# Values of batch 0 summed by matmul, and the adding transfers of batches 1 and later moved: pooled attention and two MLPs on one core

## The chip, the cores and the metric

The kernel runs on one core of one Trainium2 chip. The metric is device time in microseconds of one execution, the median over runs. In all that follows PE is the tensor engine (PEld its weight loads), DVE the vector engine, ACT the scalar engine, POOL the general engine, which also issues the transfers that add, and SP the engine that issues the other transfers. Every engine works through its own list of instructions strictly in order.

## The reference

```python
# q, k, v: [8, 8, 576, 64]; pool = 8, Sp = 72
k_p = k.reshape(B, H, Sp, pool, D).mean(axis=3)
v_p = v.reshape(B, H, Sp, pool, D).mean(axis=3)
scores = scale * np.matmul(q, k_p.transpose(0, 1, 3, 2))
attn = softmax(scores)
x = np.matmul(attn, v_p)            # tokens 4608 x 512
h = x @ moe_w_in                    # 512 x 2048
x = where(h >= 1, h, where(h <= -1, 0, (h + 1)**2 / 4)) @ moe_w_out
h = x @ moe2_w_in
out = (h / (1 + exp(-h))) @ moe2_w_out
```

All products are made of float16 pairs (a high and a low part, three matmuls each), and the weights come in as 64-bit words.

## The kernel before

The 4608 tokens are worked in nine chunks of 512. A chunk's attention makes x, then 16 slices of h (`emit_h`, twelve matmuls each), then y. Before the first slice of h can be made, `moe_w_in` has to be converted: nine pieces (`cuts1`) are loaded by SP, ACT looks at each (L237), DVE takes its maximum (L238), a matmul with the identity and a DVE reduction (L245, L248) give one scale for the whole of a group of pieces, and DVE (L92, L257, L260), ACT (L263, L265) and POOL (L266) turn a piece into its two halves `wa0` to `wa8`. A piece passes through a scratch tile `xf`, of which there are three, so the fourth conversion on DVE has to wait until POOL is done with the first.

Keys and values are pooled 8 to 1 over the rows of a batch. For batch 0's keys eight transfers bring everything, and DVE sums it (L421). All other sums of a batch (`kv_pool`) begin with a transfer of SP that brings four of the eight rows (`kv_load`, L408) into a tile `raw`, of which there are two; then a transfer issued by POOL brings the other four and adds them in place (`kv_more`, L412); then DVE adds in two steps (L427, L430) and frees `raw`. The text calls batch b's keys and values kb and vb, so v0 is batch 0's values, k1 batch 1's keys. The sums of v0 are needed early: their largest mean (L433, L106, L107) sets the scales `skv` and `tsv`, and with `tsv` ACT and DVE split x (L357, L358) for the first slice of h.

`pool_to`, `more_to` and `load_to` count through the list (k0, v0, k1, v1, ...), four pooling steps each, and are called from the main loop. The order in which an engine gets its instructions is then set by a scheduler, which moves ready work ahead by its own estimate of times; the engines keep to that order whatever the chip's times are. The row numbers of the changed file are 7 to 18 higher in the lines named here (L421 is L428, L427 and L430 are L445 and L448, L412 is L419, L571 is L589).

Of the kernel before, what the change touches and what calls it, by code (L numbers as in the profile page):

```python
# [9 lines left out]
F32 = mybir.dt.float32  # L10
# [22 lines left out]
def tile_pooled_attention_two_mlps(  # L33
# [18 lines left out]
    nc = tc.nc  # L52
    B, H, S, D = q.shape
    NT, DM = out.shape
    DFF = moe_w_in.shape[1]
    POOL = 8
    SP = S // POOL
# [42 lines left out]
    ident = const.tile([128, 128], F32, name="ident")  # L100
# [262 lines left out]
    kvp = att_ctx.enter_context(tc.tile_pool(name="kvp", bufs=4))  # L363
# [23 lines left out]
    def att_ps(shape):  # L387

        n = early["n"] % 6
        early["n"] += 1  # L390
        if early["on"] and n > 1:
            return ps_y.tile(shape, F32, tag=f"y{n - 2}", name="early")
        return ps_a.tile(shape, F32, tag="a", name="att")

    sums, kv_raw, vscale = {}, {}, {}

    def kv_rows(b, which):
        return (k if which == "k" else v)[b].rearrange("h (p r) d -> p h r d", r=POOL)

    def kv_load(b, which):  # L400
        if (b, which) == (0, "k"):
            for h in range(H):
                r = gp.tile([128, 2, N], F16, tag="g", name="k0").rearrange("p a n -> p (a n)").bitcast(F32)
                r = kv_raw[b, which, h] = r[0:SP].rearrange("p (r d) -> p r d", r=POOL)
                nc.sync.dma_start(out=r, in_=k[0, h].rearrange("(p r) d -> p r d", r=POOL))
            return
        r = kv_raw[b, which] = kvp.tile([SP, H, HALF, D], F32, tag="raw", name="raw", bufs=2)
        nc.sync.dma_start(out=r, in_=kv_rows(b, which)[:, :, 0:HALF])  # L408

    def kv_more(b, which):  # L410

        nc.gpsimd.dma_start(out=kv_raw[b, which], in_=kv_rows(b, which)[:, :, HALF:POOL], accum_op=ALU.add)  # L412

    def kv_pool(b, which, j):
        if j == 0:
            sums[b, which] = kvp.tile([SPT, H, D], F32, tag="sum", name="sum", bufs=3)
            if which == "k":
                nc.gpsimd.memset(sums[b, which][SP // 32 * 32:SPT], 0.0)
        if (b, which) == (0, "k"):  # L419
            for h in (2 * j, 2 * j + 1):  # L420
                nc.vector.tensor_reduce(  # L421
                    out=sums[b, which][0:SP, h], in_=kv_raw.pop((b, which, h)).rearrange("p r d -> p d r"),
                    axis=AX.X, op=ALU.add,
                )
        elif j == 2:
            r = kv_raw[b, which]
            nc.vector.tensor_tensor(out=r[:, :, 0:2], in0=r[:, :, 0:2], in1=r[:, :, 2:4], op=ALU.add)  # L427
        elif j == 3:  # L428
            r = kv_raw.pop((b, which))
            nc.vector.tensor_tensor(out=sums[b, which][0:SP], in0=r[:, :, 0], in1=r[:, :, 1], op=ALU.add)  # L430
# [41 lines left out]
    def values_scale(b):  # L472
        pool_to(8 * b + 8)
        if b not in vscale:
            vscale[b] = sums_scale(sums[b, "v"][0:SP], vm, ev[:, b:b + 1], rows(SP))
# [79 lines left out]
    def paced(f, engine="dve"):  # L555

        if engine in late:
            with tc.issue_after(late[engine].ins):
                f()
        else:  # L560
            f()
# [104 lines left out]
    def piece_of(cuts, m):  # L666
        return next(p for p, c in enumerate(cuts) if c[1] >= (m + 1) * 128)
# [105 lines left out]
    def emit_h(s, w, x):  # L773
        if s < KF and (s + 4) % 6 > 1:
            ps = ps_y.tile([128, N], F32, tag=f"y{(s + 4) % 6 - 2}", name="hps")
        else:
            ps = ps_h.tile([128, N], F32, tag="h", name="hps")
        wh, wl = w(s % KF)
        for c in range(KD):
            three(ps, wh[:, c], wl[:, c], x[0][:, c], x[1][:, c], c == 0, c == KD - 1)  # L780
        h_t[s] = ps
# [6 lines left out]
    def pre_A(s, r):  # L788

        w = g32_t[s] = up.tile([128, N], F32, tag="g", name="g32")  # L790
        nc.scalar.activation(out=w, in_=h_t.pop(s), func=AF.Relu, scale=c_A(r, "c1", s), bias=r["br"])  # L791

    def min_A(s, r):
        u_t[s] = up.tile([128, N], F32, tag="u", name="u")
        ts(u_t[s], g32_t[s], r["lim"], op0=ALU.min)

    def mid_A(s, r):
        nc.scalar.activation(out=u_t[s], in_=u_t[s], func=AF.Square, scale=r["rsg"])  # L798

    def post_A(s, r):  # L800

        return nc.vector.scalar_tensor_tensor(  # L802
            out=g32_t[s], in0=g32_t[s], scalar=r["br"], in1=u_t.pop(s), op0=ALU.subtract, op1=ALU.max
        )
# [21 lines left out]
    def split_g(s, r):  # L826
        g = g32_t.pop(s)
        to = slots.pop(0)() if s < KF else gp.tile([128, 2, N], F16, tag="g", name="g16")
        gh, gl = g_t[s] = to[:, 0], to[:, 1]
        nc.scalar.copy(out=gh, in_=g)  # L830
        return nc.vector.tensor_tensor(out=gl, in0=g, in1=gh, op=ALU.subtract)  # L831
# [190 lines left out]
    def batches(i):  # L1022

        b = segs(i)[-1][2]
        if i == NI:
            batch_keys(0)
            batch_values(0)
        if segs(i - 1)[-1][2] != b:
            pool_to(8 * b + 4)
            batch_keys(b)  # L1030
            pool_to(8 * b + 8)
            batch_values(b)
# [13 lines left out]


    kv = [(b, w) for b in range(B) for w in ("k", "v")]
    done = {"load": 0, "more": 1, "pool": 0, "q": 0}

    def load_to(n):
        while done["load"] < min(n, len(kv)):
            kv_load(*kv[done["load"]])
            done["load"] += 1

    def more_to(n):
        load_to(n)
        while done["more"] < min(n, len(kv)):
            kv_more(*kv[done["more"]])
            done["more"] += 1  # L1060

    def pool_to(n):
        while done["pool"] < min(n, 4 * len(kv)):
            u, j = divmod(done["pool"], 4)
            if j == 0:
                more_to(u + 1)
                load_to(u + 2)
            if done["pool"] >= 16:
                paced(lambda: kv_pool(*kv[u], j))
            else:  # L1070
                kv_pool(*kv[u], j)
            if j == 2:
                more_to(u + 2)
            done["pool"] += 1

    def q_to(n):
        while done["q"] < min(n, NTOK):
            load_q(done["q"])
            done["q"] += 1
# [4 lines left out]
    def run(*fs):  # L1084
        for f in fs:
            f()
# [1 line left out]
    load_to(1)  # L1088
    q_to(3)
    load_to(2)  # L1090
    more_to(2)
    q_to(4)
    for p in range(len(cuts1)):
        load1(p)
    load_to(3)
    pool_to(4)
    keys32(0)
    stages = [att_qT, att_scores, att_norm, att_T, att_pv]
    for n in range(NI + len(stages) - 1):
        if n == 2:  # L1100
            pool_to(8)
        for j, f in enumerate(stages):
            if 0 <= n - j < NI:
                f(n - j)
    early["on"] = False
    r = XT[0]
    for a, b in ((0, 3), (3, 7), (7, 9)):
        for p in range(a, b):
# [15 lines left out]
    def slots_to(n):  # L1124
        while left and len(first) - len(left) < n:
            with tc.high_priority(offset=1000):
                left.pop(0)()
                q_to(NI + (len(first) - len(left)) // 4 + 3)
                pool_to(16 + max(0, len(first) - len(left) - 12) * 4 // 6)

    n1 = 1
    for s in range(KF + 2):
        if s < KF:
            while n1 < min(len(cuts1), piece_of(cuts1, s) + 2):
                paced(lambda: convert1(n1), "x")
                n1 += 1
            emit_h(s, chunk1, r["x"])
        z = s - 1
        if 0 <= z < KF:
            pre_A(z, r)  # L1140
            min_A(z, r)
        if 1 <= z:
            split_g(z - 1, r)
        if 0 <= z < KF:
            mid_A(z, r)
            post_A(z, r)
        if s < 8:
            pool_to(9 + s)
        if s == 1:
            q_to(5)  # L1150
            run(*loads2)
        if s >= 9:
            slots_to((s - 8) * 6 // 8)
        if s == 12:
            run(*more2)
            run(*work2[0])
# [127 lines left out]
```

## Time and profile before

| | |
|---|---|
| median of 3 runs | 1670.01 us (1666.96 to 1671.76) |
| profiled execution | 1664.62 us, span 1662.8 us |
| busy share | PE 92%, DVE 73%, ACT 54%, POOL 34% |
| transfers | 166.35 MB, mean 100 GB/s |

The span is what the trace covers. A busy share is a mean over stages of very different kind, so what a change in one stage is worth is read from that stage alone.

### The profile page before, as it was taken

How to read it: one execution, taken by the hardware profiler on the slowest of the kernel's cores; microseconds unless marked ns; L12 is line 12 of the kernel's file. 1: busy time of each engine (PE TensorE's matmuls, PEld its weight loads, DVE VectorE, ACT ScalarE, POOL GpSimd, SP SyncE). 2: the span in 40 equal slices, each digit the busy share in tenths (PEclk: the TensorE clock that was granted, in tenths of full speed). 3: DMA queues.
4: the chain of work that ended last, by engine and by line, in shares of the span. 5: the costliest groups of instructions: out<-in, count | busy, mean ns of one | idle time of the engine just before them, and what ended most of it. 6: DMA issues, size and time to landing. Idle time of an engine off the chain costs nothing.

```text
span 1662.8 us, 34247 instructions
## 1 busy us (share of the span) xinstructions
PE 1531.8 (92%) x14214; PEld 1051.0 (63%) x14214; DVE 1215.3 (73%) x2165; ACT 892.6 (54%) x1417; POOL 570.6 (34%) x494
## 2 busy tenths in 40 slices
PE   4474779989899999999999999999999999999998
PEld 3321334444444444444444469999999999999998
DVE  6499848777667767786776757777777777777765
ACT  3277436465565656675556555445544454445543
POOL 2242321213232433341255514334334343344322
PEclk7587889989999999999999999999999999999999
DMA  9734466964737539354756241100000001000000
GB/s 286 148 104 118 95 141 165 179 147 99 129 114 122 137 79 196 80 136 110 214 212 246 100 177 40 37 27 27 27 34 33 27 27 39 27 27 27 27 15 26
DMA packets 228304, 166.35 MB, mean 100 GB/s; under 512 B 156532, under 2 KB 196340, under 8 KB 228148
## 3 DMA queue, kind: packets, MB, share of 16 engines
q1 hardware_dynamic: 216388, 155.29, 33.8%
q0 software_dynamic: 11760, 8.87, 4.2%
q8 instruction: 111, 1.82, 0.5%
q14 instruction: 45, 0.37, 0.1%
HBM read 102.76 MB, written 33.55 MB: 82 GB/s over the span
## 4 chain that ended last, share of the span: by engine, by line
PE 67%; DVE 14%; DMA 7%; ACT 6%; issue 3%; SPq 2%; POOL 1%; DVEq 0%; ACTq 0%; POOLq 0%
PE hb L119 7%; PE hb L120 7%; PE hb L121 7%; PE y L994 7%; PE y L992 7%; PE y L993 7%; PE y L119 4%; PE y L121 4%; PE y L120 4%; PE hps L119 4%; PE hps L121 4%; PE hps L120 4%; DMA kT<-rows 2%; DVE g L831 1%; DVE u L92 1%
## 5 line engine op out<-in xcount | busy, mean ns | idle before, releaser
L119 PE MATMUL hb<-xh,wc 128*128 128x128 f16 x2016 | 347.7, 219 | 0.0
L121 PE MATMUL hb<-xh,wc 128*128 128x128 f16 x2016 | 347.7, 219 | 0.0
L120 PE MATMUL hb<-xl,wc 128*128 128x128 f16 x2016 | 347.6, 219 | 0.0
L358 DVE SCALAR_TENSOR_TENSOR g<-c,tsg,g 128x512 f16<-128x512 f32 x252 | 228.7, 910 | 80.8 <-ACT g L357 80.8
L992 PE MATMUL y<-wd,g 128*128 128x256 f16 x1008 | 274.8, 273 | 0.0
L994 PE MATMUL y<-wd,g 128*128 128x256 f16 x1008 | 274.8, 273 | 0.0
L993 PE MATMUL y<-wd,g 128*128 128x256 f16 x1008 | 274.8, 273 | 0.0
L119 PE MATMUL hps<-xh,wa 128*128 128x512 f16 x576 | 224.3, 390 | 18.0 <-ACT g L791 10.8
L932 ACT ACTIVATE c<-c,tc 128x512 f32<-128x512 f32 x144 | 103.2, 717 | 228.1 <-DVE c L929 228.1
L119 PE MATMUL y<-g,wb 128*128 128x512 f16 x544 | 209.7, 388 | 16.6 <-ACT wb L210 16.1
L120 PE MATMUL hps<-xl,wa 128*128 128x512 f16 x576 | 224.1, 389 | 0.0
L357 ACT ACTIVATE g<-c,tsg 128x512 f16<-128x512 f32 x252 | 177.6, 718 | 85.7 <-POOL c L695 48.2
L121 PE MATMUL hps<-xh,wa 128*128 128x512 f16 x576 | 221.8, 386 | 1.6 <-POOL wa L266 1.5
L121 PE MATMUL y<-g,wb 128*128 128x512 f16 x544 | 210.5, 387 | 5.5 <-POOL wb L211 5.5
L120 PE MATMUL y<-g,wb 128*128 128x512 f16 x544 | 210.4, 387 | 0.5 <-DVE g L831 0.5
L929 DVE TENSOR_TENSOR c<-c,hb 128x512 f32<-128x512 f32 x252 | 168.8, 682 | 57.5 <-PE hb L121 55.3
L120 PEld LDWEIGHTS <-wc 128*128 128x128 f16 x2016 | 197.1, 98 | 2.4
L119 PEld LDWEIGHTS <-wc 128*128 128x128 f16 x2016 | 197.1, 98 | 2.3
L121 PEld LDWEIGHTS <-wc 128*128 128x128 f16 x2016 | 197.1, 98 | 0.0
L692 POOL TENSOR_TENSOR c<-c 128x512 f32<-128x512 f32 x108 | 164.0, 1532 | 2.8
L802 DVE SCALAR_TENSOR_TENSOR g<-g,tbr,u 128x512 f32<-128x512 f32 x144 | 121.0, 841 | 55.9 <-ACT u L798 55.1
L571 POOL TENSOR_TENSOR e<-e,den 128x576 f32<-128x576 f32 x36 | 52.2, 1450 | 317.0 <-DVE den L570 240.1
(180 smaller groups left out, 2701.1 us busy)
## 6 DMA issues: line engine op xcount, KB each, us to landing
raw<-in_moe_w_out_dram SPq DMA_DIRECT2D x21, 1024.0 KB
raw<-in_moe_w_in_dram SPq DMA_DIRECT2D x18, 1024.0 KB
y<-y SPq DMA_DIRECT2D x36, 256.0 KB
yin<-y SPq DMA_DIRECT2D x18, 512.0 KB
out_dram<-ob SPq DMA_DIRECT2D x36, 256.0 KB
d<-hl SPq DMA_DIRECT2D x32, 256.0 KB
qt<-in_q_dram SPq DMA_DIRECT2D x31, 256.0 KB
wc<-d SPq DMA_DIRECT2D x8, 896.0 KB
```

What stands on the lines that cost most here:

```text
L119: nc.tensor.matmul(out=acc, lhsT=wh, rhs=xh, start=start, stop=False)
L120: nc.tensor.matmul(out=acc, lhsT=wh, rhs=xl, start=False, stop=False)
L121: nc.tensor.matmul(out=acc, lhsT=wl, rhs=xh, start=False, stop=stop)
L357: a = nc.scalar.activation(out=hi, in_=x, func=AF.Copy, scale=s)
L358: return a, nc.vector.scalar_tensor_tensor(out=lo, in0=x, scalar=s, in1=hi, op0=ALU.mult, op1=ALU.subtract)
L692: nc.gpsimd.tensor_tensor(out=out, in0=a, in1=b, op=ALU.subtract)
L802: return nc.vector.scalar_tensor_tensor(out=g32_t[s], in0=g32_t[s], scalar=r["br"], in1=u_t.pop(s), op0=ALU.subtract, op1=ALU.max)
L929: nc.vector.tensor_tensor(out=out, in0=x, in1=y, op=ALU.add)
L932: nc.scalar.activation(out=x, in_=x, func=AF.Silu, scale=r["c1"])
L992: nc.tensor.matmul(out=acc, lhsT=xh, rhs=wh, start=start, stop=False)
L993: nc.tensor.matmul(out=acc, lhsT=xh, rhs=wl, start=False, stop=False)
L994: nc.tensor.matmul(out=acc, lhsT=xl, rhs=wh, start=False, stop=stop)
```

## The change

v0 is now loaded whole by SP, in four transfers into two tiles of the `raw` tag, and 32 matmuls with the identity add up the eight rows in PSUM; ACT copies the result. k1 and v1 are no longer loaded and added during the first chunk's attention: their loads are issued after it (`load_to(4)`), their adding transfers in the loop over the slices of h (`more_to(4)` at s = 1), and their pooling starts at s = 2 in place of 0. For all later batches the adding transfer is asked for one pooling step later.

```diff
         if b == 0:
+            src = v[0].rearrange("h (p r) d -> p h r d", r=POOL)
+            for j in range(2):
+                r = kv_raw[b, which, j] = kvp.tile([SP, 4, POOL, D], F32, tag="raw", name="v0", bufs=2)
+                for i in range(2):
+                    nc.sync.dma_start(out=r[:, 2 * i:2 * i + 2], in_=src[:, 4 * j + 2 * i:4 * j + 2 * i + 2])
+            return
         r = kv_raw[b, which] = kvp.tile([SP, H, HALF, D], F32, tag="raw", name="raw", bufs=2)
...
+        elif b == 0:
+            if j == 0:
+                kv_raw["ps"] = att_ps([SP, H, D])
+            ps, r = kv_raw["ps"], kv_raw[b, which, j // 2][:, j % 2 * 2:j % 2 * 2 + 2]
+            for n in range(POOL):
+                nc.tensor.matmul(
+                    out=ps[:, 2 * j:2 * j + 2], lhsT=ident[0:SP, 0:SP], rhs=r[:, :, n], start=n == 0,
+                    stop=n == POOL - 1,
+                )
+            if j == 3:
+                nc.scalar.copy(out=sums[b, which][0:SP], in_=kv_raw.pop("ps"))
...
-    done = {"load": 0, "more": 1, "pool": 0, "q": 0}
+    done = {"load": 0, "more": 2, "pool": 0, "q": 0}
...
-                load_to(u + 2)
+                load_to(u + 2 if u > 1 else 2)
...
-            if j == 2:
+            if j == 3 and u > 1:
                 more_to(u + 2)
...
     load_to(2)
-    more_to(2)
     q_to(4)
     for p in range(len(cuts1)):
         load1(p)
-    load_to(3)
     pool_to(4)
...
     early["on"] = False
+    load_to(4)
...
     for s in range(KF + 2):
+        if s == 1:
+            more_to(4)
...
-        if s < 8:
-            pool_to(9 + s)
+        if 2 <= s < 10:
+            pool_to(7 + s)
```

Three places show what this does to the order on the engines. The first is DVE at the end of the first chunk's attention, before the change: `raw_189` is k1, `raw_511` is v1, `tsv_337` the scale for x, `xl` the low half of x; what an instruction waits for stands in brackets, DMASW being the adding transfers of POOL.

```order
L107 TENSOR_REDUCE cols_95<-all_350 128x1 [waits PE_49]
L92 TENSOR_SCALAR cols_95<-cols_95 128x1 [waits DVE_49]
L94 TENSOR_SCALAR skv_348<-cols_95 128x1 [waits DVE_49]
L94 TENSOR_SCALAR te_335<-cols_95 128x1
L427 TENSOR_TENSOR raw_189<-raw_189 72x8x128 [waits DMASW1_49]
L94 TENSOR_SCALAR ts_336<-te_335 128x1 [waits DVE_49]
L94 TENSOR_SCALAR tsv_337<-te_335 128x1
L358 SCALAR_TENSOR_TENSOR v160_114<-sum_235,skv_348,v160_114 72x512 [waits Activation_49]
L430 TENSOR_TENSOR sum_513<-raw_189 72x512 [waits DVE_49,Pool_49]
L358 SCALAR_TENSOR_TENSOR xl_346<-early_358,tsv_337,xh_345 128x4x128 [waits Activation_49]
L358 SCALAR_TENSOR_TENSOR xl_346<-early_388,tsv_337,xh_345 128x4x128 [waits Activation_49]
L427 TENSOR_TENSOR raw_511<-raw_511 72x8x128 [waits DMASW2_49]
```

With the change the same scales stand in the middle of the attention, without k1 or v1 between them (DVE, a place some ten instructions earlier).

```order
L94 TENSOR_SCALAR skv_380<-cols_95 128x1 [waits DVE_49]
L94 TENSOR_SCALAR te_367<-cols_95 128x1
L585 TENSOR_SCALAR den_348<-den_348 128x8 [waits DVE_49]
L584 TENSOR_REDUCE den_401<-e_341 128x8 [waits Activation_49]
L94 TENSOR_SCALAR ts_368<-te_367 128x1 [waits DVE_49]
L94 TENSOR_SCALAR tsv_369<-te_367 128x1
```

The first steps of k1 (`raw_467`) and v1 (`raw_469`) now stand together on DVE, behind the conversion of pieces 1 and 2 of `moe_w_in` (the last L260 of which is just ahead of these rows) and ahead of the constants of the first chunk and of piece 3 (DVE again, second place, with the change).

```order
L94 TENSOR_SCALAR cols_95<-cols_95 128x2 [waits DVE_49]
L92 TENSOR_SCALAR cols_95<-cols_95 128x1 [waits DVE_49]
L445 TENSOR_TENSOR raw_467<-raw_467 72x8x128 [waits DMAHW4_49,DMAHW3_49,DMASW0_49]
L445 TENSOR_TENSOR raw_469<-raw_469 72x8x128 [waits DMAHW6_49,DMAHW5_49,DMASW1_49]
L94 TENSOR_SCALAR cols_95<-cols_95 128x2 [waits DVE_49]
L94 TENSOR_SCALAR skv_827<-cols_95 128x1 [waits DVE_49]
L681 TENSOR_REDUCE cols_95<-cols_95 128x1
L94 TENSOR_SCALAR tch_370<-cols_95,te_367 128x9
L448 TENSOR_TENSOR sum_604<-raw_467 72x512 [waits DVE_49,Pool_49]
L448 TENSOR_TENSOR sum_712<-raw_469 72x512 [waits DVE_49]
```

So the waits for k1 and v1 have moved from ahead of `tsv` to behind the first three pieces' conversion. On POOL, the third place, these are the rows between the attention and piece 3 before the change (`raw_624` is k2, `raw_1473` is v2).

```order
L412 DMA raw_189<-in_k_dram 72x8x256 [waits DMAHW6_49]
L418 MEMSET sum_513 16x512 [waits Pool_49]
L412 DMA raw_511<-in_v_dram 72x8x256 [waits DMAHW4_49,DMASW0_49,DVE_49]
L412 DMA raw_624<-in_k_dram 72x8x256 [waits DMAHW5_49,DMASW1_49,DVE_49]
L266 TENSOR_TENSOR wa0_128<-xf_448,wa0_128 128x1024 [waits Activation_49,Pool_49]
L412 DMA raw_1473<-in_v_dram 72x8x256 [waits DMAHW6_49,DMASW2_49,DVE_49]
L266 TENSOR_TENSOR wa1_129<-xf_491,wa1_129 128x1024 [waits DVE_49,Activation_49]
L266 TENSOR_TENSOR wa2_130<-xf_541,wa2_130 128x1024 [waits DVE_49,Activation_49]
```

And these with the change, where `raw_467`, `raw_469`, `raw_710` and `raw_1508` are k1, v1, k2 and v2.

```order
L419 DMA raw_467<-in_k_dram 72x8x256 [waits DMAHW5_49,DMAHW4_49,DMAHW3_49]
L419 DMA raw_469<-in_v_dram 72x8x256 [waits DMAHW6_49]
L266 TENSOR_TENSOR wa0_128<-xf_484,wa0_128 128x1024 [waits Activation_49]
L266 TENSOR_TENSOR wa1_129<-xf_527,wa1_129 128x1024 [waits DVE_49,Activation_49]
L419 DMA raw_710<-in_k_dram 72x8x256 [waits DMAHW1_49,DMASW0_49,DVE_49]
L425 MEMSET sum_1510 16x512 [waits DVE_49,Pool_49]
L266 TENSOR_TENSOR wa2_130<-xf_575,wa2_130 128x1024 [waits Activation_49,Pool_49]
L419 DMA raw_1508<-in_v_dram 72x8x256 [waits DMAHW2_49,DMASW1_49]
```

The adding transfers of k1 and v1 now follow each other at once, and the low halves of pieces 2 and 3 stand behind those of k2 and v2. On SP the loads of k1 and v1 now come behind all of `moe_w_in` and the next four loads of q, and ahead of the first two pieces of `moe_w_out`. Behind this stage POOL's list is the same but for one swap, and PE's list is the same row for row over its last nine tenths.

## Rows read from the trace of the kernel before

**Rows 1.** Busy time by stage: start:end, length, engines busy (instructions), granted clock, DMA share, GB/s.

```profile
0.00:45.00 45.00, 17.77 (x96) 14.45 (x96) 28.14 (x48) 17.39 (x24) 10.32 (x16) 0.76 0.95 278
45.00:60.00 15.00, 4.56 (x22) 3.13 (x22) 1.05 (x5) 2.76 (x7) 2.74 (x3) 0.50 0.91 193
60.00:78.20 18.20, 10.44 (x54) 7.60 (x55) 13.25 (x27) 6.36 (x9) 4.07 (x3) 0.50 0.58 113
78.20:118.60 40.40, 32.35 (x144) 14.35 (x143) 39.24 (x63) 25.20 (x35) 18.50 (x8) 0.92 0.41 109
118.60:160.00 41.40, 17.57 (x88) 7.26 (x86) 40.65 (x94) 32.29 (x54) 6.17 (x3) 0.75 0.43 119
160.00:215.00 55.00, 42.35 (x261) 18.98 (x262) 42.70 (x70) 26.86 (x38) 22.00 (x15) 0.81 0.49 109
215.00:420.00 205.00, 184.76 (x1187) 88.67 (x1186) 142.54 (x296) 111.55 (x193) 54.57 (x49) 0.94 0.70 143
420.00:1662.80 1242.80, 1221.97 (x12370) 896.56 (x12368) 907.66 (x1569) 670.15 (x1062) 452.25 (x399) 1.00 0.30 84
```

**Rows 2.** Waits of DVE from 40 to 165 us: total, times, longest.

```profile
DVE raw L427 <- DMA raw<-in_k_dram: 12.5, 1, 12.5
DVE cols L107 <- PE all L106: 9.4, 1, 9.4
DVE raw L427 <- DMA raw<-in_v_dram: 4.9, 1, 4.9
```

**Rows 3.** Timeline of DVE: start, duration, instruction, idle before it.

```profile
59.67 1.22 DVE L427 TENSOR_TENSOR raw<-raw 72x1024 f32<-72x1024 f32 x1 [12.51 <-DMA raw<-in_k_dram]
...
68.47 1.22 DVE L427 TENSOR_TENSOR raw<-raw 72x1024 f32<-72x1024 f32 x1 [4.88 <-DMA raw<-in_v_dram]
...
71.14 0.68 DVE L430 TENSOR_TENSOR sum<-raw 72x512 f32<-72x512 f32 x1
...
71.74 0.74 DVE L358 SCALAR_TENSOR_TENSOR xl<-att,tsv,xh 128x512 f16<-128x512 f32 x1
...
72.40 0.67 DVE L238 TENSOR_SCALAR_CACHE_REDUCE wa<-wa 128x512 f32<-128x512 f32 x1
...
78.16 2.16 DVE L92 TENSOR_SCALAR xf<-wa 128x1024 int32<-128x1024 int32 x3
...
80.85 1.21 DVE L257 SCALAR_TENSOR_TENSOR xf<-raw,xf 128x1024 int32<-128x1024 int32 x1
...
83.79 1.21 DVE L260 SCALAR_TENSOR_TENSOR xf<-raw,xf 128x1024 int32<-128x1024 int32 x1
...
86.06 0.41 DVE L248 TENSOR_REDUCE cols<-all 128x2 f32<-128x256 f32 x1
...
118.57 1.21 DVE L180 TENSOR_SCALAR_CACHE_REDUCE xf<-xf 128x1024 f32<-128x1024 f32 x1
```

**Rows 4.** Timeline of ACT: its looks at pieces 5 and 8 of `moe_w_in`.

```profile
34.54 1.14 ACT L237 ACTIVATE wa<-wb 128x1024 f32<-128x1024 f32 x1 [1.47 <-DMA wb<-in_moe_w_in_dram]
...
43.76 1.12 ACT L237 ACTIVATE wa<-wb 128x1024 f32<-128x1024 f32 x1 [2.33 <-DMA wb<-in_moe_w_in_dram]
```

**Rows 5.** Timeline of POOL: it issues the adding transfers of k1 and v1.

```profile
47.62 1.40 POOL L412 DMA_DIRECT2D raw<-in_k_dram  x1 [11.22 <-DMA raw<-in_k_dram]
...
59.18 1.38 POOL L412 DMA_DIRECT2D raw<-in_v_dram  x1 [9.59 <-DMA raw<-in_v_dram]
```

**Rows 6.** Transfers, 46 to 75 us: adding queue's packets, MB, share of 16 engines.

```profile
q0 software_dynamic: 1568, 1.18, 28.7%
```

**Rows 7.** Transfers, 0 to 40 us: issues, count, KB each, us to landing (v0).

```profile
raw<-in_v_dram POOLq DMA_DIRECT2D x1, 576.0 KB, 13.4
```

**Rows 8.** Transfers, 70 to 100 us: the same for k2 and v2.

```profile
raw<-in_k_dram POOLq DMA_DIRECT2D x1, 576.0 KB, 9.9
...
raw<-in_v_dram POOLq DMA_DIRECT2D x1, 576.0 KB, 7.8
```

**Rows 9.** Groups of PE up to 60 us: busy us, mean ns; idle before.

```profile
L453 PE MATMUL att<-ident,sum 72*128 72x72 f32 x4 | 1.4, 360 | 7.6 <-DVE sum L421 7.6
```

More of the change, by code (lines that the diff above doesn't have):

```diff
@@ L406, in kv_load @@
             return
+        if b == 0:
+            src = v[0].rearrange("h (p r) d -> p h r d", r=POOL)
[4 more added lines that the diff above has]
+            return
         r = kv_raw[b, which] = kvp.tile([SP, H, HALF, D], F32, tag="raw", name="raw", bufs=2)
```

## The prediction

> **What bounds the kernel now.** I read the table of stages first [rows 1]. From 420 us on PE is busy 1222 of 1243 us at the full clock; nothing in the change touches that stretch, so it can only start sooner or later. The part ahead of it is where time can be won. Up to 45 us the transfers set the pace (share 0.95): nine pieces of moe_w_in come in, one MB each 3.07 us (pieces 5 to 8, 34.54 to 43.76 [rows 4]). From 45 to 60 us nothing works: DVE is busy 1.05 of 15 us, PE 4.56, ACT 2.76. From 78.2 to 160 us DVE is busy 79.9 of 81.8 us, while PE is busy 49.9: DVE converts the weights, and PE waits for them. So the first 160 us are a chain of loads, then waits, then DVE, and what DVE loses there the whole kernel loses.
>
> Next I read what DVE waited for [rows 2]: 12.5 us for the adding transfer of k1 and 4.9 us for that of v1. Nobody needs k1 or v1 yet; but the wait for k1 stands ahead of tsv in DVE's list, so x, the scales and the conversion of pieces 1 to 8 stand behind it. The third wait, 9.4 us, ends with v0's maximum, shortly after the last piece. The timeline [rows 3] shows the consequence: six maxima (L238) start only at 72.40, although the last piece was read by ACT from 43.76 [rows 4], and the conversion of piece 1 starts at 78.16.
>
> **What the change removes.** By the order, tsv and the four splits of x no longer wait for k1 or v1. With v0 whole at PE in the first 20 us, the attention of chunk 0 goes on as before up to about 40 us, and DVE takes the maxima as the pieces come. From about 40 us it has to do, in this order: four splits of 0.74, six maxima (72.40 to 78.16, 5.8), then what stood from 78.16 to 86.06 and a little behind it, less the half-width piece 3, which now comes later. From the rows: L92 and L248, 78.16 to 80.85 less 0.4 for piece 3, 2.3; two L257 of 1.21, 2.4; two L260, 83.79 to 86.06, 2.3; small ones some 1.5, an estimate [rows 3]. That is 3.0 + 5.8 + 8.5 = 17.3, so DVE stands at about 57.4 us before the first step of k1.
>
> **The wait that it adds.** There DVE waits again: L445 of k1 and of v1 need both adding transfers. When do they land? Half of v0 (0.59 MB) moves from an adding transfer to a plain one. Two adding transfers took 28.7% of sixteen engines over 29 us [rows 6], so 4.2 us each; plain, the same bytes take 1.8 us at 3.07 us per MB [rows 4]. So moe_w_in is in about 2 us sooner, at 41.7. Behind it come four loads of q (0.79 MB) and the halves of k1 and v1 (1.18 MB), 6.0 us at that pace, 47.7; I take 49.5, since SP issues them late. (Before, k1's half was in at 47.62 and v1's by 59.18 [rows 5].) POOL issues in 1.4 us. Alone or in traffic one such transfer took 12.05 us (k1: 47.62 to 59.67), 9.3 (v1: 59.18 to 68.47 [rows 3, 5]), 13.4 (v0 [rows 7]), 9.9 and 7.8 (k2, v2 [rows 8]). Here two run together with one to two MB of moe_w_out: 2 x 4.2 + 3.1 to 6.1 = 11.5 to 14.5 us if all sixteen engines are kept busy. The later one lands at 49.5 + 1.4 + 13 = 64 us. Lower bound: 49.5 + 1.4 + 7.8 = 58.7, beyond which DVE's own 57.4 counts. Upper bound: one behind the other at the largest durations, 50.9 + 12.05 + 13.4 = 76.4. I take 64, as the engines' share in such stretches was 0.91 [rows 1] and so the work, not the latency, decides.
>
> Behind that wait on DVE stand the constants of the chunk (without which ACT can't empty PSUM), batch 0's keys, and pieces 3 to 8; PE meanwhile has the converted pieces 0 and 1 and the high half of piece 2, so it can fill PSUM, but that buys nothing, since DVE is the bound.
>
> The Trainium skill, DMA: Bandwidth & Descriptors, section on the anatomy of one DMA on the SWDGE path, gives 2.0 us plus bytes over 436 GB/s for a transfer issued by GpSimd: 3.4 us for 0.59 MB. The trace disagrees (7.8 to 13.4 us for five adding ones). By that page of the Trainium skill the later one would be in at about 54, ahead of DVE, and the wait would be gone; the sum would give 1647 in place of 1653.
>
> **From the wait on.** A place that both kernels pass in the same state is the first L180, the first maximum of moe_w_out: 118.57 us before [rows 3]. From 78.16 to it passed 40.4 us. With the change the part behind the wait lacks the 7.0 us named above (2.3 + 2.4 + 2.3), and has in addition the first step of v1 and both second steps, 1.22 + 2 x 0.68 = 2.6 [rows 3]; the first step of k1 fits into the wait. That is 36.0. POOL adds something: the low half of piece 2 stands behind k2's adding transfer, whose load can only start when raw is free, some 2.4 us after the landing, and DVE's next use of that xf tile waits for it. The load (1.8 us at the pace of rows 4, and a start), POOL's issue of 1.4 and its own work end about 11 us after the landing, when DVE has come there at about 9. I take 2 us, between 0 (a wait of the size of the idle that the 40.4 us held anyway, 40.40 less 39.24 [rows 1]) and 6 (load and issue in full). So L180 starts at 64 + 38.0 = 102.0 in place of 118.6: **16.6 us sooner**.
>
> **What costs nothing.** 32 matmuls for v0: the nearest row is 360 ns for 72 partitions [rows 9], 11.5 us at most if none overlapped; PE is busy 17.8 of the first 45 us, and all wait for pieces until 43.76. Without that cover up to 11.5 us less whatever lies under v0's own load would show; I take 0. ACT's copy of the sum, under the 1.12 us of rows 4, lies there too. The two DVE steps of v0 (1.9 us) go, from a stretch in which DVE is idle 16.9 of 45 us [rows 1]: 0. The later batches' transfers asked for a step later: POOL's list behind the first stage is the same, so 0; the bounds are a microsecond or two either way.
>
> **What becomes of it.** From 118.6 to 160 us DVE stays full, so all of the gain is handed on. From 160 to 420 us PE is busy 227 of 260 us [rows 1], with waits that come from the conversion and transfers of the same chunks; they move with the rest. Sum: 1664.6 - 16.6 = 1648.0 for the profiled execution. That one lies 5.4 us under the median of the runs shown and 2.3 under the fastest, so I carry the difference over to the median: 1670.0 - 16.6 = **1653 us**.
>
> **Rivals.** All times are medians. (a) *No wait left*: the adding transfers are in by 57.4, or DVE comes there later than I think. Then L180 starts at 57.4 + 38 = 95.4, 23 us sooner: 1647. For it: sixteen engines may be freer than before, and 58.7 is my lower bound; against: not one of the five landed in under 7.8 us. The Trainium skill, on the page cited above, would have it so. (b) *Half is lost later*: in the conversion of moe_w_out (160 to 215 us) DVE is only busy 42.7 of 55 us, so ACT, POOL and loads share the bound, and a shorter start may leave them behind: 8 us left, 1662. Against: the loads of moe_w_out wait for tiles that DVE frees, and so come sooner as well. (c) *No change*: the later adding transfer lands at 76.4, the upper bound; then L180 starts at 114.4, 4 us sooner, 1666, or the later stages eat it all, 1670. For it: 13.4 us in the heaviest traffic [rows 7]. (d) *Slower*: the two adding transfers and the plain loads share the engines so badly that the landing is later than 118.6 - 38.0 = 80.6 us, 31 us after the loads; each us beyond costs one, and from 85.6 the loss is over 0.3%, say 1676. For it: everything of DVE, and by xf and POOL's list everything of POOL, hangs on this one landing; against: it is six us more than the worst sum of rows.
>
> **How the numbers follow.** My case (landing between 60 and 69, 1649 to 1658) has 0.50, (a) 0.18, (b) 0.13, (c) 0.12, (d) 0.07. 0.3%, 5 us, is about what a measurement of this kernel can tell from no change (its three runs span 4.8). The forecast, (a) and (b) are beyond it: faster 0.81, same 0.12, slower 0.07. The range from 1643 (a with some luck behind it) to 1665 (between b and c) leaves out (d), most of (c) and little else.
>
> **What would show it.** Right: no DVE wait for k1 or v1 ahead of the splits of x; the last piece's maximum soon after 44 to 46 us; one wait of DVE for the adding transfer of v1, 4 to 8 us, ending near 64; POOL's low half of piece 2 some 11 us behind it; the first L180 near 102; the stretch behind it as long as before. Wrong: a landing beyond 70, a DVE that arrives much before or after 57, a wait of DVE on POOL over 6 us, or a first L180 that is early and a last PE instruction that is not.

## The result, and the profile after

The changed kernel takes 1652.12 us (median of 4 runs, 1646.63 to 1653.79); the kernel before took 1668.49 beside it (4 runs, 1666.14 to 1671.76). The ratio is 0.9895, with a 95% interval of 0.9864 to 0.9926: 16.4 us faster. The profiled execution took 1653.58 us, its span is 1651.8, so only 11.0 us below that of before; the table at the end of the experiments comes back to the rest.

The changed kernel's table of stages, columns as in [rows 1]:

```profile
0.00:45.00 45.00, 29.41 (x220) 25.32 (x220) 29.53 (x58) 24.68 (x38) 8.55 (x16) 0.89 0.93 281
45.00:60.00 15.00, 3.56 (x14) 2.54 (x14) 13.39 (x29) 1.93 (x2) 2.91 (x2) 0.62 0.98 209
60.00:78.20 18.20, 8.58 (x31) 3.39 (x31) 9.66 (x23) 7.36 (x12) 7.65 (x5) 0.78 0.77 159
78.20:118.60 40.40, 33.75 (x135) 14.57 (x136) 35.24 (x60) 31.11 (x47) 18.04 (x8) 0.86 0.56 140
118.60:160.00 41.40, 18.50 (x105) 8.02 (x104) 37.08 (x78) 29.73 (x47) 8.78 (x5) 0.71 0.36 89
160.00:215.00 55.00, 45.35 (x335) 21.65 (x332) 42.15 (x70) 24.34 (x33) 24.43 (x16) 0.91 0.38 103
```

Against [rows 1] the second line tells most: from 45 to 60 us DVE is busy 13.39 us in place of 1.05. The third gives some of it back, 9.66 in place of 13.25, and in the fourth and fifth DVE is no longer full (72.3 of 81.8 us, 79.9 before). The waits of DVE from 0 to 165 us, columns as in [rows 2]:

```profile
DVE u L92 <- ACT g L809: 7.3, 2, 5.6
DVE raw L445 <- DMA raw<-in_v_dram: 4.5, 1, 4.5
DVE wa L238 <- ACT wa L237: 4.5, 1, 4.5
DVE xl L358 <- ACT xh L357: 4.2, 1, 4.2
DVE xf L180 <- ACT xf L175: 3.2, 1, 3.2
...
DVE raw L445 <- DMA raw<-in_k_dram: 1.6, 1, 1.6
```

The three waits of [rows 2], 26.8 us, have gone from their places; 6.1 us for k1 and v1 stand at the new place, and waits for ACT have come in. DVE's timeline shows where, columns as in [rows 3]:

```profile
35.42 0.14 DVE L94 TENSOR_SCALAR tsv<-te 128x1 int32<-128x1 int32 x1
...
44.63 0.68 DVE L238 TENSOR_SCALAR_CACHE_REDUCE wa<-wa 128x512 f32<-128x512 f32 x1
...
58.08 0.15 DVE L92 TENSOR_SCALAR cols<-cols 128x1 int32<-128x1 int32 x1
59.84 1.22 DVE L445 TENSOR_TENSOR raw<-raw 72x1024 f32<-72x1024 f32 x1 [1.61 <-DMA raw<-in_k_dram]
65.60 2.00 DVE L445 TENSOR_TENSOR raw<-raw 72x1024 f32<-72x1024 f32 x1 [4.54 <-DMA raw<-in_v_dram]
...
80.09 2.61 DVE L92 TENSOR_SCALAR u<-g,tlim 128x512 f32<-128x512 f32 x1 [5.64 <-ACT g L809]
...
107.00 1.22 DVE L180 TENSOR_SCALAR_CACHE_REDUCE xf<-xf 128x1024 f32<-128x1024 f32 x1 [3.19 <-ACT xf L175]
```

tsv is there at 35.42 (60.88 before), the maxima start at 44.63 (72.40 in [rows 3]), DVE is through with the first pieces at 58.2, v1 lands at 65.60, and the first L180 comes at 107.00, 11.6 us sooner than before. What held DVE at 80 us shows in the timeline of ACT:

```profile
77.53 0.63 ACT L451 ACTIVATE rows<-sum 80x512 f32<-80x512 f32 x1 [4.07 <-DMA kT<-rows]
...
79.29 0.76 ACT L809 ACTIVATE g<-hps,tbr,tc 128x512 f32<-128x512 f32 x1
```

ACT takes k1's mean (L451) and writes the output that nobody needs into a `rows` tile, which the transposes of the keys (kT) still read; g, for which DVE waits, stands behind it.

A later common place is the first DVE step on the first chunk's y, which waits for the chunk's last matmul. It comes at 228.92 us before and at 213.04 after:

```profile
228.92 1.41 DVE L92 TENSOR_SCALAR y<-y,cy 128x512 f32<-128x512 f32 x2 [2.40 <-PE y L121]
```

```profile
213.04 1.41 DVE L92 TENSOR_SCALAR y<-y,cy 128x512 f32<-128x512 f32 x2 [2.40 <-PE y L121]
```

There the gain is 15.9 us. The table at the end of the experiments uses this place.

### The profile page after: what moved, and what is told of

The parts are those of the page before. It is cut to its first block, busy times and chain, and to the rows that moved or that the text cites. A ratio compares the mean times of both kernels' runs of the same rounds, so it can differ in the third digit from the quotient of the medians.

```text
span 1651.8 us, 34386 instructions
## 1 busy us (share of the span) xinstructions
PE 1536.8 (93%) x14278; PEld 1055.8 (64%) x14278; DVE 1203.7 (73%) x2163; ACT 894.3 (54%) x1418; POOL 572.1 (35%) x493
## 4 chain that ended last, share of the span: by engine, by line
PE 52%; DVE 13%; DMA 11%; issue 9%; ACT 7%; POOL 6%; SPq 1%; DVEq 0%; POOLq 0%; ACTq 0%
PE y L119 5%; PE y L120 5%; PE y L121 5%; PE hps L121 5%; PE hps L120 5%; PE hps L119 5%; PE y L1010 4%; POOL c L710 4%; PE y L1011 4%; PE y L1012 4%; PE hb L121 3%; PE hb L120 3%; PE hb L119 3%; DMA kT<-rows 3%; DMA yin<-y 2%
```

## The experiments

**v0_only**: the kernel before with the v0 part alone, that is, with the new branches of `kv_load` and `kv_pool` and these lines.

```diff
-    done = {"load": 0, "more": 1, "pool": 0, "q": 0}
+    done = {"load": 0, "more": 2, "pool": 0, "q": 0}
...
     load_to(2)
-    more_to(2)
```

> The kernel before with the v0 part of the change alone: v0 is loaded whole and summed by matmul, while the calls that load, add and pool k1 and v1 stay where they were. By the order of instructions the list of every engine is then that of the changed kernel, row for row but for tile numbers. Theory: the gain comes from v0's sum alone, because with it tsv stands ahead of k1's and v1's waits on DVE; 1649 to 1655 us, ratio 0.987 to 0.993, first L180 at 105 to 109 us. Rival: it is the later loading and pooling of batch 1 that frees the stage; then this kernel would be at 0.997 or above.

Measured: 1646.32 us, ratio 0.9873 (0.985 to 0.9897), first L180 at 105.64. Its timeline of DVE repeats the changed kernel's, a microsecond sooner throughout:

```profile
58.73 1.22 DVE L445 TENSOR_TENSOR raw<-raw 72x1024 f32<-72x1024 f32 x1 [1.53 <-DMA raw<-in_k_dram]
64.64 1.93 DVE L445 TENSOR_TENSOR raw<-raw 72x1024 f32<-72x1024 f32 x1 [4.69 <-DMA raw<-in_v_dram]
```

So the v0 part alone does it: with it the scheduler gives the same order, wherever the code asks for k1 and v1. The two kernels have one list of instructions, and their medians still differ by 5.8 us with overlapping intervals; taken together their eight runs, which are of two rounds, have the median 1648.0. They are called the pooled runs below.

**late_only**: the change without its v0 part; the new branches of `kv_load` and `kv_pool` are taken out of the changed kernel.

```diff
-    done = {"load": 0, "more": 2, "pool": 0, "q": 0}
+    done = {"load": 0, "more": 1, "pool": 0, "q": 0}
...
     load_to(2)
+    more_to(2)
```

> The changed kernel without its v0 part: v0 comes in by half, is added by POOL and summed by DVE as before, while the loads, adding transfers and pooling of k1 and v1 stand where the change puts them. By the order k1's first step still stands ahead of tsv on DVE. Theory: no gain, 1664 to 1675 us, first L180 at 116 to 121 us, and a DVE wait of 9 to 14 us for k1 or v1 ahead of the splits of x. Rival: the later calls are what helps: 1650 to 1660 us.

Measured: 1666.68 us, ratio 0.9998 (0.9982 to 1.0013). The order of every engine is that of the kernel before, and so is DVE's timeline:

```profile
59.73 1.22 DVE L427 TENSOR_TENSOR raw<-raw 72x1024 f32<-72x1024 f32 x1 [12.35 <-DMA raw<-in_k_dram]
...
118.50 1.21 DVE L180 TENSOR_SCALAR_CACHE_REDUCE xf<-xf 128x1024 f32<-128x1024 f32 x1
```

The later calls for k1, v1 and the later batches do nothing in either direction.

**add_twice**: v1's adding transfer is issued twice.

```diff
-        nc.gpsimd.dma_start(out=kv_raw[b, which], in_=kv_rows(b, which)[:, :, HALF:POOL], accum_op=ALU.add)
+        for _ in range(2 if (b, which) == (1, "v") else 1):
+            nc.gpsimd.dma_start(out=kv_raw[b, which], in_=kv_rows(b, which)[:, :, HALF:POOL], accum_op=ALU.add)
```

> The changed kernel, but POOL issues v1's adding transfer twice (four of v1's eight rows are counted twice). The second stands right behind the first, so v1 lands about one such transfer later; the five of the kernel before took 7.8 to 13.4 us, which puts v1's landing at 73 to 79 us in place of 65.6. Theory: DVE waits for it and each us of landing costs a us, less the constants of the chunk (under 2 us), which by the order now stand ahead of v1's first step: first L180 at 112 to 119 us in place of 107.0, 1655 to 1664 us. Rival: the waits of DVE for ACT (5.64 us) and for POOL (3.19 us) that stand behind the landing in the changed kernel take the lateness up, since they end by other chains; first L180 at 107 to 110 us, 1648 to 1655 us.

Measured: 1657.73 us, ratio 0.9933 (0.9909 to 0.9957). POOL issues the second one at 64.74, after waiting 11.01 us for the first, and DVE gets v1 at 73.17:

```profile
73.17 1.22 DVE L446 TENSOR_TENSOR raw<-raw 72x1024 f32<-72x1024 f32 x1 [11.28 <-DMA raw<-in_v_dram]
...
109.31 1.20 DVE L180 TENSOR_SCALAR_CACHE_REDUCE xf<-xf 128x1024 f32<-128x1024 f32 x1
```

The landing is 7.6 us later, the first L180 only 2.3 us, as the rival said: DVE's waits for ACT and POOL took part of it up (4.08 us in place of 5.64, none in place of 3.19). But the step on y comes at 220.50, 7.5 us later, and the median is 5.6 us above the changed kernel's and 9.7 above the pooled 1648.0 (by ratio its interval still touches that of the change). So by the end of the chunk a later landing is paid nearly in full, as the theory said, and the first L180 was the wrong place to read it. The second transfer also holds POOL's own list: its low halves begin at 65.58 in place of 62.31, and how much of the 7.5 us is theirs wasn't separated.

**no_add_1**: no adding transfers for batch 1, so four of the eight rows are left out of k1 and v1.

```diff
     def kv_more(b, which):
+        if b == 1:
+            return
```

> The changed kernel without the adding transfers of batch 1: four of the eight rows of k1 and v1 are left out of their sums. In the changed kernel DVE waited 1.6 us for k1's and 4.5 us for v1's. Theory: nothing else ends that wait, since POOL saw the plain loads landed at 50.6 and 53.4 us and DVE comes at 58.2; all 6.1 us come back, first L180 at 100 to 102 us, 1644 to 1648 us, ratio to before 0.985 to 0.988. Rival: the transposes of the keys, POOL's low halves or the loads of moe_w_out take over; the two waits are gone but L180 comes at 104 us or later, 1650 us or more.

Measured: 1651.67 us, ratio 0.9915 (0.9888 to 0.9942), first L180 at 104.77, the step on y at 214.44. The waits for k1 and v1 are gone, and the list of DVE's waits has a new first row:

```profile
DVE xf L92 <- POOL wa L266: 8.5, 1, 8.5
```

The rival holds. The edit also moved something that I hadn't meant to: with POOL's list shorter, k2's and v2's adding transfers stand ahead of all low halves, and the first of these began at 72.29 (62.31 in the changed kernel). It shows what is late next, but it doesn't price the landing alone.

**pool_behind_4**, **pool_behind_7**, **behind_7_psum**: the pooling of k1 and v1 moved behind later pieces on DVE, so that nothing waits for a landing; `cv` is the last L260 so far. The diff is that of pool_behind_7; pool_behind_4 pools two slices of h sooner, behind_7_psum has the edit of psum_junk (below) as well.

```diff
             if done["pool"] >= 16:
+            if 8 <= done["pool"] < 16:
+                paced(lambda: kv_pool(*kv[u], j), "cv")
+            elif done["pool"] >= 16:
...
-        if 2 <= s < 10:
-            pool_to(7 + s)
+        if 6 <= s < 14:
+            pool_to(3 + s)
```

> The changed kernel, with the pooling of k1 and v1 put behind the conversion of pieces 3 and 4 on DVE (and v1's behind pieces 5 and 6), so DVE passes the place at 58 to 66 us without a wait; k2's adding transfer then stands behind five low halves on POOL in place of two. Theory: the landing of k1 and v1 (6.1 us of waits) and what stood behind it is lost time: the last step of piece 8 (the last L260) comes 6 to 12 us sooner than in the changed kernel, 1638 to 1646 us. Rival: POOL and ACT take over, as their low halves and casts (2.1 and 1.1 us a piece) are handed to DVE in order: under 3 us sooner, 1646 us or more.

> The same, with k1's and v1's pooling behind pieces 6 and 7, and k2's and v2's adding transfers behind eight low halves on POOL. Theory: as the kernel before it, and a little better, since the transposes of k1's rows, for which ACT waited 4.07 us in the changed kernel, then fall behind nearly all of the conversion: the last L260 8 to 14 us sooner than in the changed kernel, 1635 to 1645 us. Rival: batch 1's keys and values come too late for the second chunk's attention, and the gain is given back there: 1646 us or more, with PE less busy from 118 to 215 us than in the changed kernel.

> The same as the kernel before it, and k1's mean on ACT also writes its unused output to PSUM, so that it doesn't wait for the transposes. Theory: with the pooling that late ACT's wait for the transposes falls into a stretch where DVE is still the bound, so this adds 0 to 3 us to the gain: 1634 to 1644 us. Rival: it adds nothing (within 1 us of the kernel before it), or PSUM, with one tile more to hold, makes an emptying wait and costs 1 to 3 us.

Measured: 1654.66 us (0.991, 0.9884 to 0.9936), 1649.04 (0.9877, 0.9854 to 0.990) and 1645.87 (0.9862, 0.9838 to 0.9885). The step on y comes at 213.81, 214.40 and 213.38: not sooner than in the changed kernel. DVE's waits from 55 us on in pool_behind_7 show no landing any more, and small waits for ACT and POOL in its place:

```profile
DVE xf L180 <- ACT xf L175: 3.2, 1, 3.2
DVE xf L92 <- POOL wa L266: 2.4, 1, 2.4
DVE rows L358 <- ACT rows L357: 2.2, 1, 2.2
```

With add_twice this says where the bound lies: later than 65.6 us the landing costs, sooner than that it brings nothing. What the traces show just behind it is DVE's own work and its exchange with ACT and POOL. None of the three came into the range of its theory (1638 to 1646, 1635 to 1645 and 1634 to 1644 us); the last L260, which was to come 6 to 14 us sooner in the first two, came at 99.87 and 99.69 (102.00 in the changed kernel). By ratio the intervals of all three overlap those of the change and of v0_only; by medians pool_behind_4 is 6.7 us above the pooled 1648.0.

**psum_junk**: the unused output of k1's mean goes to PSUM.

```diff
-        s = sums_scale(x, km, ek[:, b:b + 1], lo)
+        s = sums_scale(x, km, ek[:, b:b + 1], att_ps([SPT, H * D]) if b == 1 else lo)
```

> The changed kernel, but the mean of k1 on ACT (L451) writes the output that nobody reads into a PSUM tile and not into the rows tile, so it doesn't wait for the transposes of the keys that read that tile. In the changed kernel ACT waited 4.07 us there, and DVE then 5.64 us for ACT's g. Theory: this wait is a loss of its own behind the landing of v1; first L180 2 to 5 us sooner than in the changed kernel (102 to 105 us), 1647 to 1650 us. Rival: behind it stand POOL (conversion steps of 3 to 9 us, and k2's adding transfer), and DVE and ACT then wait for these: L180 and time as in the changed kernel within 1 us.

Measured: 1650.35 us, ratio 0.9902 (0.9877 to 0.9927), first L180 at 105.93, the step on y at 214.75. ACT's wait for the transposes is gone and DVE's longest wait for g with it (1.5 us is left); in its place DVE waits elsewhere:

```profile
DVE g L820 <- ACT u L816: 5.0, 2, 4.3
...
DVE xf L92 <- POOL wa L266: 2.0, 1, 2.0
```

The first of these is 4.3 us long and stands at 142.76 us, behind L180. The edit also changed the order: ACT takes k1's mean at 67.7 us in place of 77.53, and the lists of ACT and DVE behind it are others. The time can't tell theory from rival; the step on y, no sooner than in the changed kernel, speaks for the rival: the most visible wait behind the landing was worth nothing that shows.

**after_k2_late**: k2's and v2's adding transfers behind later low halves on POOL, in the changed kernel; `pl` is the last L266 so far. order_k2_late below has the same edit.

```diff
+        def add():
+            nc.gpsimd.dma_start(out=kv_raw[b, which], in_=kv_rows(b, which)[:, :, HALF:POOL], accum_op=ALU.add)
+
+        paced(add, "pl") if b == 2 else add()
```

> The same edit in the changed kernel: k2's and v2's adding transfers behind the low halves of pieces 6 and 8 on POOL, in place of those of pieces 1 and 2; nothing else. The prediction took 2 us (0 to 6) for what they cost DVE by way of POOL. Theory: the low half of piece 2 came at 76.65 us, behind k2's issue at 74.62, and nothing of DVE waited for POOL longer than 1 us there, so the last L198 moves by less than 2 us (163.5 to 166 us) and the time stays at 1646 to 1653 us. Rival: they hold the conversion back: last L198 at 162 us or sooner, under 1646 us.

Measured: 1648.4 us, ratio 0.9891 (0.985 to 0.9932); first L180 at 102.88, the step on y at 211.29. The theory holds: it is worth nothing that can be measured. The times that the expectations give for the last L198 are those of the fifth of eight; the fifth comes at 163.57 here (165.53 in the changed kernel), the last at 192.98 (194.72, and 193.37 in v0_only).

**order_only**, **order_behind_7**, **order_k2_late**: v0 as before the change, and DVE's order changed by hand, so that k1 and v1 stand behind the conversion of the pieces made so far (in order_behind_7 behind pieces 6 and 7). POOL's order changes with it: v2's adding transfer, behind one low half before, stands behind seven in order_only. The diff is order_only's, against late_only.

```diff
+            if 8 <= done["pool"] < 16:
+                paced(lambda: kv_pool(*kv[u], j), "cv")
+            elif done["pool"] >= 16:
```

> The kernel before in its v0 part (half loaded, added by POOL, summed by DVE), with the later calls for k1 and v1 of the change and one thing more: k1's and v1's steps on DVE are put behind the conversion of the pieces made so far. So tsv, the splits of x and the maxima no longer stand behind k1's or v1's wait, although v0 comes no sooner; the wait of DVE for v0's maximum, 9.4 us before, stays. Theory: what the change gains is only this order. DVE gets tsv at about 47 us, passes splits, six maxima and three pieces in about 19 us, and comes to k1's first step at about 66 us, after its landing, with no wait for k1; the last step of moe_w_out's conversion (the last L198, 178.74 us before, 165.53 in the changed kernel) comes at 161 to 167 us, 1648 to 1654 us, ratio 0.986 to 0.991. Rival: the early sum of v0 by matmul, which gives tsv 10 us sooner, is needed; then the last L198 comes at 170 us or later, 1656 us or more.

> The same, with the steps of k1 and v1 behind pieces 6 and 7. Theory: no wait for an adding transfer is left, and nothing else is changed, so it is as the kernel before it or up to 3 us faster: last L198 at 158 to 166 us, 1645 to 1654 us. Rival: the waits of DVE for POOL's low halves grow by what is taken away: within 1 us of the kernel before it, or slower.

> The kernel order_only, with the adding transfer of k2 (and with it v2's) put behind the low half of piece 6 on POOL. In order_only the first L180 came 14.3 us sooner than before, but the last L198 only 5.9 us and the end 0.5 us sooner; between them POOL stood 6.5 us at v2's adding transfer, the low half behind it took 7.21 us, ACT then waited 5.49 us for POOL and DVE 5.33 us for ACT. Theory: POOL's list is where order_only gives its gain back: without those transfers in it the last L198 comes at 162 to 169 us, 1650 to 1658 us. Rival: the loss lies elsewhere (v0's late sum shifts ACT's and PE's share of the first slices into the conversion of moe_w_out): last L198 at 171 us or later, 1660 us or more.

Measured: 1666.16 us (0.9995, 0.998 to 1.001), 1657.78 (0.9947, 0.9926 to 0.9968) and 1659.8 (0.9959, 0.994 to 0.9978). This is where I was most wrong. In order_only DVE no longer waits for k1 or v1, as the theory said, but it comes to k1's first step at 72.82 in place of about 66: v0's maximum is late, and five waits for PE and ACT, 5.0 us in all, follow between tsv and the maxima. The first L180 is 14.3 us sooner than before, 2.7 sooner than in the changed kernel:

```profile
48.00 0.29 DVE L107 TENSOR_REDUCE cols<-all 128x1 f32<-128x128 f32 x1 [10.96 <-PE all L106]
...
58.55 0.68 DVE L238 TENSOR_SCALAR_CACHE_REDUCE wa<-wa 128x512 f32<-128x512 f32 x1
...
104.29 1.20 DVE L180 TENSOR_SCALAR_CACHE_REDUCE xf<-xf 128x1024 f32<-128x1024 f32 x1
...
117.00 0.75 DVE L802 SCALAR_TENSOR_TENSOR g<-g,tbr,u 128x512 f32<-128x512 f32 x1 [5.33 <-ACT u L798]
```

But the step on y comes only 5.0 us sooner and the end 0.5 us. A part of the loss can be followed in the timelines of POOL and ACT, and ends in DVE's wait at 117.00:

```profile
105.56 1.42 POOL L412 DMA_DIRECT2D raw<-in_v_dram  x1 [6.54 <-DVE xf L180]
106.44 7.21 POOL L266 TENSOR_TENSOR wa<-xf,wa 128x1024 f16<-128x1024 f32 x1
```

```profile
113.69 1.12 ACT L175 ACTIVATE xf<-raw 128x1024 f32<-128x1024 f32 x1 [5.49 <-POOL wa L266]
```

POOL stands at v2's adding transfer (the view names L180 as what released it; the plain load that the transfer also needs was issued only at 99.6, when DVE was through with v1), its low half behind that is late, ACT waits for it, and DVE for ACT. order_k2_late takes the transfer from that place: the wait at 117 us disappears, the step on y comes at 219.78, and 6 us of the median come back. The rest, 11.8 us of medians to the pooled 1648.0, goes with the early sum of v0. What that sum is worth with k1 and v1 out of the way, two kernels above show: pool_behind_7 and order_behind_7 differ in the v0 part alone, and are at 0.9877 (0.9854 to 0.99) and 0.9947 (0.9926 to 0.9968), with the step on y at 214.40 and 225.95.

So order_only's rival holds; order_behind_7, faster than order_only by intervals that don't meet, and order_k2_late fell between theory and rival. Here too the expectations' marks are those of the fifth L198, which came at 172.80, 176.56 and 171.13. The last one came at 208.09 before, at 194.72 in the changed kernel, and at 204.25, 207.34 and 200.32 in these three; from it to the step on y it took 18.3 to 20.9 us in every kernel of this document, so it would have been a good mark.

The kernels by the same places, us; gains against the kernel before (L180 isn't comparable where the list around it was changed, marked *):

| kernel | first L180 | DVE busy up to 60 us | step on y, gain | span, gain | ratio |
|---|---|---|---|---|---|
| before | 118.57 | 29.18 | 228.92 | 1662.8 | |
| late_only | 118.50 | 29.11 | 228.67, 0.3 | 1665.2, -2.4 | 0.9998 |
| order_only | 104.29* | 35.17 | 223.91, 5.0 | 1662.3, 0.5 | 0.9995 |
| order_k2_late | 105.65* | 34.89 | 219.78, 9.1 | 1660.0, 2.8 | 0.9959 |
| order_behind_7 | 108.10* | 34.38 | 225.95, 3.0 | 1653.6, 9.2 | 0.9947 |
| add_twice | 109.31* | 43.57 | 220.50, 8.4 | 1655.2, 7.6 | 0.9933 |
| no_add_1 | 104.77* | 44.50 | 214.44, 14.5 | 1648.5, 14.3 | 0.9915 |
| the change | 107.00 | 42.92 | 213.04, 15.9 | 1651.8, 11.0 | 0.9895 |
| v0_only | 105.64 | 44.02 | 211.73, 17.2 | 1646.4, 16.4 | 0.9873 |

From the step on y to the end of the span it is 1433.9 us before and 1436.5 in late_only, 1438.8 after and 1434.7 in v0_only: the same list gives figures some 4 us apart. So the 4.9 us by which the one profiled pair (11.0) falls short of the gain at y (15.9) is little more than two executions of one list differ by, and can't be put down to the change.

## Why the prediction came out

**Right.** The place and the kind: with v0 summed by matmul, tsv and the maxima don't stand behind k1's and v1's waits, and DVE's idle time ahead of 60 us shrinks from 30.8 to 17.1 us. DVE came to k1's first step at 58.2 (57.4 foretold), the loads were in at 50.61 and 53.43 (49.5), the later transfer landed at 65.60 (64; its bounds were 58.7 and 76.4), the wait was 4.5 us, and POOL's low half of piece 2 came 11.05 us behind the landing (11). Rival (a) did not happen, nor did the late landings of (c) and (d). From issue at 53.43 to DVE's start it took 12.2 us. So the trace again disagrees with the estimate of 3.4 us worked out from the Trainium skill, DMA: Bandwidth & Descriptors, section on the anatomy of one DMA on the SWDGE path. The 32 matmuls, 64 rows of the trace from 16.03 us on, took 7.2 us, against the 11.5 that I gave as the most (columns as in [rows 9]):

```profile
L437 PE MATMUL early<-v,ident 72*72 72x128 f32 x64 | 7.2, 272 | 0.0
```

They and the copy cost nothing that shows: ACT came to the last piece at 43.83 (43.76 before). Whether the pieces were in 2 us sooner, at 41.7, that row doesn't say, as ACT didn't wait for it. The later calls cost 0 (late_only). Rival (d) was said to lie six us beyond the worst sum of rows; 80.6 less 76.4 is 4.2.

**Off in size.** From the landing to the first L180 I counted 36.0 us of DVE work and 2 us of waiting for POOL; there were 41.4 us, 32.3 busy and 9.1 idle. The work was overcounted by 3.7 us, and the term of 2 us, bounded by 0 and 6, held 9.1: 5.64 for ACT behind the keys' transposes, 3.19 for ACT behind POOL's low half, and nothing for POOL itself. So L180 was 5.0 us later than foretold. And the sentence that all of the gain is handed on as it stands at L180 was wrong by nearly as much the other way: from L180 to the step on y it took 106.0 us in place of 110.4. From the first y matmul to its end 63.5 us went by in place of 67.4, with PE idle 10.1 us in place of 12.7 (at a mean granted clock of 0.88, 0.86 before) and POOL busy 28.8 in place of 30.5. DVE was busy 88.9 of the 106.0 us in place of 92.7 of 110.4, so what shrank is mostly busy time; why was not tested, and the steps between the two places aren't quite the same. The gain was 11.6 us at L180 and 15.9 at y, where 16.6 was forecast for both: the sum is right partly by luck, because two errors of 4 to 5 us cancel. That 1652.12 lies within 1 us of the 1653 is luck as well: v0_only, with the same list, has 1646.32.

**What the argument lacked.** I wrote as if the wait for k1 ahead of tsv were the whole matter and the early v0 only the way to get rid of it. order_only takes that wait away and leaves v0 late, and gains nothing: DVE still waits 11.0 us for v0's maximum, the maxima start at 58.55 (44.63 in the changed kernel, 72.40 before), and what it wins at L180 is lost in part to the chain over POOL and ACT (a loss of the kind of rival (b), which the change itself escaped).

Nor is the gain all idle time of DVE, in which the prediction counted it. Up to the step on y DVE has the same steps to do but for the two of v0. Here is that stretch before and with the change, columns as in [rows 1]:

```profile
0.00:228.92 228.92, 137.31 (x742) 71.42 (x742) 174.33 (x312) 116.07 (x172) 72.63 (x52) 0.78 0.58 145
```

```profile
0.00:213.04 213.04, 137.91 (x810) 74.51 (x812) 165.21 (x310) 117.31 (x173) 70.37 (x51) 0.82 0.60 157
```

DVE's idle time falls from 54.6 to 47.8 us, by 6.8: of the 13.7 us that were won ahead of 60 us, 7.0 came back as waits behind it, those for k1 and v1 among them, and DVE, full from 60 to 160 us before (93.1 of 100 us), is busy only 82.0 there. The other 9.1 us of the gain of 15.9 are busy time: v0's two steps, 2.7 us, for which the prediction put 0, and some 6.4 us by which the same steps took less time, for which it had no term. Some took longer (the sixteen L92 on u 864 ns in place of 721), more took less. An example, before and after, a group of four steps with its busy time and the mean of one in ns:

```profile
L257 DVE SCALAR_TENSOR_TENSOR xf<-wb,xf 128x1024 int32<-128x1024 int32 x4 | 6.7, 1694 | 0.0
```

```profile
L257 DVE SCALAR_TENSOR_TENSOR xf<-wb,xf 128x1024 int32<-128x1024 int32 x4 | 4.9, 1217 | 0.0
```

In all kernels with a late v0 DVE is busy 174.1 to 176.3 us up to the step on y, in all with the early one 165.2 to 170.5. What shortens the steps was not tested; the last section has a candidate. What order_k2_late and order_behind_7 do behind y stays open: order_behind_7 gains less at y (3.0) than at the end (9.2).

## What to carry to other kernels

Price an early wait at a place where the bound engine's full stretch has ended, and count idle and busy time up to there: of 13.7 us of idle time won early, 7.0 came back as other waits, and the first row behind the edit moved by 14.3 us in a kernel that was no faster. Taking away the most visible wait paid only while nothing stood close behind it; here neither the landing (6.1 us) nor ACT's wait (5.6 us) brought anything that shows, though a later landing came with a loss of nearly its full length. An edit that changes when one thing is ready can make a scheduler reorder several engines, so look at the order first: the later calls of this diff changed no order at all, and they did nothing.

## What the runs showed of the hardware that was not expected

Some short DVE steps are drawn out while POOL computes. In the changed kernel the L92 at 80.09 us took 2.61 us, where the same step alone takes 0.47, and it ended at 82.7, just after a pair of POOL's low halves (79.60, 2.80 us). In order_only two short DVE steps, the first on 128x4, took 2.17 us at 73.95 (0.16 for one on 128x4 elsewhere) beside POOL's L266. POOL in turn took some 15.80 us (spans on POOL are rough) for two low halves in order_behind_7, which take 2.1 us each when undisturbed; DVE was busy all that time:

```profile
91.08 15.80 POOL L266 TENSOR_TENSOR wa<-xf,wa 128x1024 f16<-128x1024 f32 x2 [4.46 <-ACT wa L265]
```

The Trainium skill, SBUF — State Buffer, section on the two separate sides, says that a GpSimd operation and certain VectorE operations share a port pair and that the one that starts first holds it for the whole instruction. The first two cases agree; in the third POOL loses far more than the length of one DVE step, which that sentence alone doesn't explain. Work moved beside POOL can so be worth less than its own length; how much of the 9.1 us of waits and of the 6.4 us of shorter steps this made was not measured.
